# Attention row maxima: four of 32 per unit as a + relu(b - a), single-bank PSUM tiles, and a table of ten phases

## The chip, the core and the metric

The kernel runs on one core of one Trainium2 chip. The metric is the device time of one execution in microseconds (us). Before the change it is 5757.02 us, the median of three runs (5755.38 to 5757.16). The profile is of one further execution, which took 5756.38 us.

## The reference

Four transformer-like layers, A, B, A, B, over a sequence of 2048 rows of 576 values. Each layer adds to x the attention of its normalised input; 32 heads have 18 values each. In layers B all heads share one key and one value head. All is fp32.

```python
def _A_ref(x, wqkv, wo):                    # S = 2048, D = 576, H = 32, Dh = 18
    qkv = (x @ wqkv).reshape(B, S, 3, H, Dh).transpose(2, 0, 3, 1, 4)
    q, k, v = qkv[0], qkv[1], qkv[2]
    scores = jnp.einsum("bhqd,bhkd->bhqk", q, k) * (Dh ** -0.5)
    p = _softmax(scores, axis=-1)
    o = jnp.einsum("bhqk,bhkd->bhqd", p, v)
    return o.transpose(0, 2, 1, 3).reshape(B, S, D) @ wo
x = A_x
x = x + _A_ref(_layernorm(x), A_wqkv, A_wo)
x = x + _B_ref(_layernorm(x), B_wq, B_wk, B_wv, B_wo)   # k, v: one head for all 32
...                                                     # both once more
```

## The kernel before, in words

**Stages of a layer.** Each layer normalises x, projects it to q, k and v on TensorE, runs the attention loop, and projects the result out. Projections split every fp32 operand into a high and a low part and multiply them in TensorE's fp32r format. The attention loop takes most of the time: the 64 **units** of a layer, a unit being one pair of heads `p` (16 pairs) and one block `u` of 512 queries (4 blocks). The instruction order is written out by hand and each engine runs its own queue in that order.

**What a unit does.** The two heads of a pair lie on partitions 0 to 63 (head 0) and 64 to 127 (head 1), so that matmuls of the two heads use different row halves of TensorE's array and run side by side. A unit has

- 32 **m** matmuls (`max_mm`, line 553): 128 queries by 512 keys of one head into PSUM, only to find each query's largest score. VectorE reduces them (line 562). Two m matmuls fill the two banks of one tile `psm` of 1024 columns, and one VectorE instruction takes the maxima of both.
- `max_final` (line 691): the 32 columns of partial maxima (8 query blocks of 4) become 8 negated maxima (VectorE, line 693), split into two parts on GpSimd (`hl`, lines 144 and 697); `max_store` transposes them on VectorE (line 702) and sends them to DRAM, and `max_rows` (line 708) brings them into two spare rows of the query operand in `big`.
- 32 **e** matmuls (`exp_mm`, line 717): 128 keys by 512 queries, with the two spare rows, so that the score minus its maximum comes out. ScalarE takes the exponential (line 721).
- the **PV** matmuls (`pv_block`, line 742): the probabilities times the values, four at a time in four column groups of the array, into one accumulator bank `oacc`. A unit has 4096 columns of them (8 blocks of 512, each for four tiles of probabilities). ScalarE then copies `oacc` out once (line 749), and GpSimd (lines 144, 759, 768, 781) normalises.

**Order.** The maxima of a unit run `LEAD` = 14 steps ahead of its exponentials (a step is an eighth of a unit, 4 m and 4 e). A table `UNIT` gives one period of TensorE's order: each **phase** lists m and e matmuls with their heads, and then a number of PV columns. The table of before has twelve phases. `run_todo` places the small work (DMAs on SyncE's queue, GpSimd steps, loads of the next pair and of later weights) at numbered steps. The first 56 m of a layer are woven into the end of its projections; after its last m, 56 e are left and run without m.

**PSUM.** There are eight banks: two tiles of two banks with tag `m` (`mtile2`), three single banks with tag `e`, and `oacc`. The projections use the same tags; where they want one bank they take the first half of an m tile.

**Staging of weights.** `load_w` brings raw weights into a tile `raw`, and GpSimd splits them one step later (lines 144, 170). In the loop `raw` comes from the two buffers of tag `xh`, in turn.

Of the kernel before, what the change touches and what calls it, by code (L numbers as in the profile page):

```python
# [17 lines left out]
DH = D // H  # L18
# [4 lines left out]
SCALE = DH ** -0.5  # L23

# [38 lines left out]

UNIT = [("m0 m1 e0 e0 e1 m0 m1", 384), ("e0 m1 m0 e1 e0", 352), ("m0 m1 e1 e0 e1 m0 m1", 320), ("m1 e0 e1 m0", 256),
        ("m1 e0 m1 e0 e1", 416), ("e1 m0 m0 e1 m1 e0", 416), ("e1 m0 m1 e0 e1 m0", 384), ("e0 e1 m0 m1 e0", 256),
        ("m1 e0 m0 e1", 128), ("e1 m0 m1 e0", 192), ("e1 m0 m1 e0", 416), ("m0 m1 e1 e0 e1 m1 m0", 576)]
UNIT = [([(o[0], int(o[1])) for o in rows.split()], cols) for rows, cols in UNIT]


@with_exitstack  # L70
def tile_kernel(ctx: ExitStack, tc: tile.TileContext, A_x, A_wqkv, A_wo, B_x, B_wq, B_wk, B_wv, B_wo, out):
# [31 lines left out]
    vbuf = cst.tile([P, NV], F32, name="vbuf")  # L103
    xx = cst.tile([P, 2, 9, 256], F32R, name="xx")
    oacc = psum.tile([P, 512], F32, name="oacc")
    mark = cst.tile([P, 1], F32, name="mark")

# [4 lines left out]
    qk_d = dram.tile([2 * D, 3, S], F32, name="qk_d")  # L112

# [33 lines left out]
    def load_w(c, dsts, srcs, n, hi, lo, spare, raw=None):  # L147


        if raw is None:  # L150
            raw = pool.tile([P, 640], F32, tag="xh", bufs=2, name="raw") if spare else ptile("raw")
# [134 lines left out]
    def out_w(c):  # L286
        ot = ots_[c // 2][:, :, c % 2 * P:(c % 2 + 1) * P]
        ps = mtile2("psn")
        for h in range(2):
            natural(ot, h, ps[:, h])  # L290
        xc = xo[:, c, :].rearrange("p (h n) -> p h n", h=2)
        nc.vector.tensor_tensor(xc, ps[:, :, :288], xc, op=OP.add)
# [85 lines left out]
    for layer in range(4):  # L378
# [11 lines left out]
        def project(T, t, filler=False, half=None, terms=TERMS):  # L390
            t0 = T * 512
            n = 114 if not is_a and t == 4 else P
            if t in half_done:
                ps = half_done.pop(t)
            elif half == 0 and t == 2:
                ps = pair_of[0][:, 1]
            elif half == 0:
                pair_of[t] = mtile2("psq")
                ps = pair_of[t][:, 0]
            else:  # L400
                ps = (etile if filler else mtile)("psq")
# [41 lines left out]
        vts, half_done, pair_of = [], {}, {}  # L443
# [8 lines left out]
        def project_v(c):  # L452
            ps = mtile2("psn")
            for h in range(2):
                natural(xt_of(c), h, ps[:, h])
            return ps[:, :, :288].rearrange("p h (e d) -> p h e d", d=DH)
# [58 lines left out]
        m_open, m_next, m_done, m_count, m_full = [], [0, 0], [0], {}, []  # L515
# [5 lines left out]

        def max_place(a, i):
# [4 lines left out]
            return p, u, i // 2 % 4, i // 8 % 2 * 2 + i % 2  # L527
# [4 lines left out]
        m_banks, n = [], [0, 0]  # L532
        for i in range(0, 4 * ns, 2):
            at_ = []
            for a in m_heads[i:i + 2]:
                p, u, qc, kb = max_place(a, n[a])
                at_.append((p, u, 16 * a + 4 * qc + kb))
                n[a] += 1
            m_banks += [0, 1] if at_[0] < at_[1] else [1, 0]

        def max_mm():

            a, slot = m_heads[m_done[0]], m_banks[m_done[0]]
            p, u, qc, kb = max_place(a, m_next[a])
            q, k = ops(p)
            if (p, u) not in mxs:
                mxs[p, u] = pool.tile([P, 32], F32, name="mx")
            if m_done[0] % 2 == 0:
                m_open.append((mtile2("psm"), []))
            ps, rows = m_open[0]  # L550
            b = 64 * a
            c0 = u * 512 + qc * P
            nc.tensor.matmul(ps[:, slot], q[b:b + KM, c0:c0 + P], k[b:b + KM, kb * 512:(kb + 1) * 512],  # L553
# [344 lines left out]
```

## Time and profile before

| what | value |
|---|---|
| median of three runs | 5757.02 us |
| the profiled execution | 5756.38 us |
| its span (first to last instruction) | 5754.6 us |
| mean granted TensorE clock | 0.998 |
| m matmuls, of 512 columns | 8192 |
| reductions of 1024 columns (line 562) | 4096 |
| exponentials of 512 columns (line 721) | 8192 |

A row of the profile's groups names line, engine, operation, the tiles and shapes, the count, the busy time, the mean duration of one instruction, and the idle time of the engine just before. Instructions of one engine overlap: the busy time counts overlapped time once, so that count times mean can be more than the busy time. TensorE is PE, VectorE DVE, ScalarE ACT, GpSimd POOL, SyncE SP. In a timeline, rows of one group that follow each other are merged: start, length of the merged stretch, and the count behind the x. A PV row of x8 is four fp32 matmuls, each recorded twice.

### The profile page before, as it was taken

The numbers are of one execution on the slowest core, as the hardware profiler recorded it, in microseconds if no ns is written. First come the engines' busy times: TensorE is split into PE (matmuls) and PEld (weight loads), VectorE is DVE, ScalarE is ACT, GpSimd is POOL, SyncE is SP. The second block draws the span as 40 slices with busy tenths as digits, with TensorE's granted clock in tenths as the row PEclk, the third lists the DMA queues.
The fourth block names the chain that finished last, engine by engine and source line by source line (L and its number), as shares of the span: only waits on it lengthen the run. The fifth ranks groups of instructions, "written<-read, shape, count | busy, mean of one in ns | idle before, by whom it ended". The sixth has DMA issues, their size and how long they took to land.

```text
span 5754.6 us, 140964 instructions
## 1 busy us (share of the span) xinstructions
PE 5724.3 (99%) x57758; PEld 2917.8 (51%) x57758; DVE 5121.0 (89%) x5330; ACT 4576.9 (80%) x8864; POOL 1731.4 (30%) x2224
## 2 busy tenths in 40 slices
PE   9999999999999999999999999999999999999999
PEld 8644444444844444444686444444448444444446
DVE  4799999998699999999637999999977999999995
ACT  2588888888378888888625888888882888888885
POOL 3133232323233232323311323232342332323232
PEclk9999999999999999999999999999999999999999
DMA  6311111110420000001243111111114101010002
GB/s 201 106 46 32 35 32 36 32 33 22 127 66 23 23 22 21 20 23 24 59 166 95 40 36 32 36 32 36 29 28 135 52 22 23 22 24 19 23 14 78
DMA packets 250482, 276.93 MB, mean 48 GB/s; under 512 B 131748, under 2 KB 172196, under 8 KB 240116
## 3 DMA queue, kind: packets, MB, share of 16 engines
q1 hardware_dynamic: 249836, 267.92, 16.9%
q8 instruction: 453, 7.42, 0.6%
q14 instruction: 193, 1.58, 0.1%
HBM read 151.24 MB, written 112.56 MB: 46 GB/s over the span
## 4 chain that ended last, share of the span: by engine, by line
PE 97%; POOL 1%; DVE 1%; DMA 1%; ACT 0%; SPq 0%; issue 0%; POOLq 0%; ACTq 0%; DVEq 0%
PE oacc L742 37%; PE pse L717 24%; PE psm L553 23%; PE psn L224 6%; PE psq L405 6%; DVE mx L562 0%; PE ps L216 0%; DMA raw<-in_B_wk_dram 0%; ACT pt L721 0%; POOL big L170 0%; SPq L157 0%; PE oacc L217 0%; POOL os L781 0%; DMA raw<-in_A_wqkv_dram 0%; POOL os L759 0%
## 5 line engine op out<-in xcount | busy, mean ns | idle before, releaser
L562 DVE TENSOR_REDUCE mx<-psm 128x2 f32<-128x1024 f32 x4096 | 4735.7, 1218 | 177.0 <-PE psm L553 161.3
L721 ACT ACTIVATE pt<-pse 128x512 f32<-128x512 f32 x8192 | 4289.5, 606 | 527.1 <-PE pse L717 389.6
L553 PE MATMUL psm<-big 62*128 62x512 f32 x8192 | 2540.9, 452 | 4.2 <-DVE mx L562 3.7
L717 PE MATMUL pse<-big 64*128 64x512 f32 x8192 | 2491.3, 433 | 7.7 <-DMA big<-m_d 5.5
L742 PE MATMUL oacc<-pt,vbuf 128*19 128x64 f32 (+6 forms) x27536 | 1777.8, 361 | 3.5 <-DVE oc L144 3.5
L717 PEld LDWEIGHTS pse<-big 64*128 64x128 f32 x8192 | 1221.7, 184 | 875.9 <-ACT pt L721 700.9
L553 PEld LDWEIGHTS psm<-big 62*128 62x128 f32 x8192 | 1054.0, 184 | 813.4 <-DVE mx L562 640.3
L742 PEld LDWEIGHTS oacc<-pt,vbuf 128*19 128x19 f32 x27536 | 535.4, 97 | 768.5 <-issue 590.9
L144 POOL TENSOR_SCALAR hl<-neg 128x8 fp32r<-128x8 f32 x256 | 50.5, 197 | 2630.8 <-DVE neg L693 2630.8
L768 POOL TENSOR_TENSOR rl<-lt,mone 128x8 f32<-128x8 f32 x256 | 422.1, 1649 | 578.8 <-DMA lt<-os 578.7
L742 PE MATMUL oacc<-pt,vy 128*19 128x128 f32 (+3 forms) x9168 | 594.3, 362 | 0.0
L144 POOL TENSOR_SCALAR os<-oc 32x512 f32<-32x512 f32 x512 | 313.0, 611 | 126.5 <-DVE oc L144 72.5
L781 POOL TENSOR_TENSOR os<-os,rb 96x512 f32<-96x512 f32 x256 | 329.3, 1286 | 21.2 <-DMA rb<-r_d 20.4
L759 POOL TENSOR_TENSOR os<-os,oc 96x512 f32<-96x512 f32 x256 | 328.0, 1281 | 21.3
L742 PEld LDWEIGHTS oacc<-pt,vy 128*19 128x19 f32 x9168 | 195.6, 98 | 271.6 <-issue 212.0
L413 ACT ACTIVATE ev<-psq 128x512 fp32r<-128x512 f32 (+1 forms) x112 | 66.9, 598 | 326.3 <-PE psq L405 236.7
L224 PE MATMUL psn<-wsm,xx 128*128 128x288 f32 x2240 | 307.8, 296 | 0.1
L224 PEld LDWEIGHTS psn<-wsm,xx 128*128 128x128 f32 x2240 | 298.6, 188 | 11.5 <-issue 7.8
L419 DVE TENSOR_TENSOR ev<-psq,ev 128x512 fp32r<-128x512 f32 (+1 forms) x84 | 58.0, 691 | 215.7 <-ACT ev L413 197.4
L405 PE MATMUL psq<-yx,big 128*128 128x512 f32 (+2 forms) x826 | 197.5, 392 | 5.1 <-DVE ev L419 2.5
L405 PE MATMUL psq<-xx,big 128*128 128x512 f32 (+1 forms) x784 | 194.0, 397 | 0.0
L405 PEld LDWEIGHTS psq<-yx,big 128*128 128x128 f32 (+1 forms) x826 | 146.9, 190 | 39.7 <-issue 3.0
(75 smaller groups left out, 1390.5 us busy)
## 6 DMA issues: line engine op xcount, KB each, us to landing
big<-qk_d SPq DMA_DIRECT2D x180, 432.0 KB
qk_d<-ev SPq DMA_DIRECT2D x96, 512.0 KB
qk_d<-ev SPq DMA_DIRECT2D x120, 256.0 KB
rb<-r_d SPq DMA_DIRECT2D x512, 36.0 KB
o_d<-os SPq DMA_DIRECT2D x512, 36.0 KB
m_d<-tr SPq DMA_DIRECT2D x1024, 2.0 KB
o<-o_d SPq DMA_DIRECT2D x64, 256.0 KB
big<-m_d SPq DMA_DIRECT2D x512, 4.0 KB
```

What stands on the lines that cost most here:

```text
L144: eng.tensor_scalar(dst, src, 1.0, 0.0, op0=OP.mult, op1=OP.add)
L224: nc.tensor.matmul(ps, lhs[:, xc, :], wsm[:, wc, h * 288:(h + 1) * 288], start=i == 0, stop=i == len(TERMS) - 1)
L405: nc.tensor.matmul(ps[:n].rearrange("p (u t) -> p u t", u=2)[:, us], w[:, wc, :n], xts[T][:, us, xc, :], start=(xc, wc) == TERMS[0], stop= ...
L413: nc.scalar.activation(ev[0][:n], ps[:n], AF.Copy)
L553: nc.tensor.matmul(ps[:, slot], q[b:b + KM, c0:c0 + P], k[b:b + KM, kb * 512:(kb + 1) * 512], start=True, stop=True)
L562: nc.vector.reduce_max(mxs[p, u][:, r0:r1 + 1:r1 - r0], ps, axis=AX.X)
L717: nc.tensor.matmul(e, k[r:r + KE, kc * P:(kc + 1) * P], q[r:r + KE, u * 512:(u + 1) * 512], start=True, stop=True)
L721: nc.scalar.activation(pt, e, AF.Exp, scale=SCALE)
L742: nc.tensor.matmul(oacc[j:j + DH + 1, cs], v_of(kc)[:, 2 * p + a if is_a else 0, :], pts[p, u, i][:, cs], start=kc < 2 and c0 == 0, stop=k ...
L759: nc.gpsimd.tensor_tensor(t[:96], t[:96], oc[:96], op=OP.add)
L768: nc.gpsimd.tensor_tensor(rl, lts.pop((p, u)), mone, op=OP.pow)
L781: nc.gpsimd.tensor_tensor(t[:96], t[:96], rb[:96], op=OP.mult)
```

## The change

- **Maxima by pairs.** For pairs p > 0, four of the 32 m of a unit (places 9, 16, 24 and 31 of the table's cycle of 32, `UNIT_X`) no longer compute scores of key block 1. They multiply the queries with `kd`, the difference of key block 1 and key block 0, so that PSUM holds b - a. ScalarE writes relu(b - a) into one SBUF tile `relu`. When the scores a of key block 0 of the same queries come, VectorE adds the two and takes the maximum in one call, `tensor_tensor_reduce`, which the built program has as two instructions: one over 512 columns, and one that writes a 128x1 result. It stands for two reductions. The other 24 m of a unit are reduced one by one, 512 columns each. For p = 0 all 32 are. So a unit with p > 0 has 24 reductions of 512, 4 of the new pairs of instructions, and 4 relus.
- **The difference of the keys**, once for each pair in layers A and once in layers B: four DMAs in, five GpSimd instructions on 256 columns, three DMAs out and two back in, at four steps of the loop, into the tile `xx`, which is otherwise unused there.
- **Banks.** Tag `m` becomes three tiles of one bank, tag `e` four, and `oacc` keeps one. Projections use single banks; some VectorE and ScalarE instructions on 576 columns become two on 288.
- **The table** has ten phases. m, e and PV columns of a unit are in sum 32, 32 and 4096, as before.
- **Staging.** The second `xh` buffer is now the one `raw` tile for all weights loaded in the loop, because the first holds `relu`.

```diff
-UNIT = [("m0 m1 e0 e0 e1 m0 m1", 384), ("e0 m1 m0 e1 e0", 352), ("m0 m1 e1 e0 e1 m0 m1", 320), ("m1 e0 e1 m0", 256),
-        ("m1 e0 m1 e0 e1", 416), ("e1 m0 m0 e1 m1 e0", 416), ("e1 m0 m1 e0 e1 m0", 384), ("e0 e1 m0 m1 e0", 256),
-        ("m1 e0 m0 e1", 128), ("e1 m0 m1 e0", 192), ("e1 m0 m1 e0", 416), ("m0 m1 e1 e0 e1 m1 m0", 576)]
+UNIT = [("m1 e0 e1 e0 m1 m0", 512), ("m0 e1 m1 e0 e1 m0", 480), ("e1 m0 m1 e0 e0 m0 e1", 416),
+        ("m1 m0 e1 e0 e1 m0", 224), ("e1 m0 m1 m1 e0", 544), ("m1 m0 e0 e1 e1 m0", 352), ("e0 m1 e1 m0 e0 m1", 416),
+        ("m0 e1 e1 m1 e0 m1 e0", 384), ("m1 m0 e1 e0 m0 e0 e1 m1 m0", 448), ("m0 e1 m1 e0 m1 e0", 320)]
+UNIT_X = (9, 16, 24, 31)
...
-    def mtile2(name):
-        return psum.tile([P, 2, 512], F32, tag="m", bufs=2, name=name)
     def mtile(name):
-        return mtile2(name)[:, 0]
+        return psum.tile([P, 512], F32, tag="m", bufs=3, name=name)
     def etile(name):
-        return psum.tile([P, 512], F32, tag="e", bufs=3, name=name)
+        return psum.tile([P, 512], F32, tag="e", bufs=4, name=name)
...
         def max_mm():
...
+            if p > 0 and (a, qc, kb) in m_diff:
+                nc.tensor.matmul(ps, q[b:b + 3 * DH, c0:c0 + P], kd(p)[b:b + 3 * DH], start=True, stop=True)
+                t = relus[p, u, a, qc] = relu[:, :512]
+                nc.scalar.activation(t, ps, AF.Relu)
+            else:
+                nc.tensor.matmul(ps, q[b:b + KM, c0:c0 + P], k[b:b + KM, kb * 512:(kb + 1) * 512], start=True, stop=True)
+                if kb == 0 and (p, u, a, qc) in relus:
+                    t = relus.pop((p, u, a, qc))
+                    nc.vector.tensor_tensor_reduce(t, ps, t, 1.0, LOWEST, OP.add, OP.max, mx[:, r:r + 1])
+                else:
+                    nc.vector.reduce_max(mx[:, r:r + 1], ps, axis=AX.X)
...
-                nc.vector.reduce_max(mxs[p, u][:, r0:r1 + 1:r1 - r0], ps, axis=AX.X)
...
+        def diff_split(p):
+            n = 4 * DH if is_a else 2 * DH
+            d = dif[:n]
+            hi0, hi1, lo0, lo1 = (xx_flat.bitcast(F32)[:n, 1024 + 256 * i:1280 + 256 * i] for i in range(4))
+            hi, lo = (xx_flat[:n, 2048 + 256 * i:2304 + 256 * i] for i in range(2))
+            nc.gpsimd.tensor_tensor(d, hi1, hi0, op=OP.subtract)
+            nc.gpsimd.tensor_tensor(d, d, lo1, op=OP.add)
+            nc.gpsimd.tensor_tensor(d, d, lo0, op=OP.subtract)
+            copy(nc.gpsimd, hi, d)
+            nc.gpsimd.tensor_tensor(lo, d, hi.bitcast(F32), op=OP.subtract)
...
+        relu, raw = (pool.tile([P, 640], F32, tag="xh", bufs=2, name=n) for n in ("relu", "raw"))
...
+            if p + 1 < NPAIR and (is_a or p == 0):
+                b = max(LEAD, 32 * p - 10)
+                for d, f in ((0, diff_in), (3, diff_split), (5, diff_out), (8, diff_rows)):
+                    at(b + d, f, p + 1)
...
-                at(b - 30, load, c, (2,), nc.gpsimd, nc.gpsimd, True)
-                at(b + 2, load, c, (0,), nc.gpsimd, nc.gpsimd, True)
+                at(b - 30, load, c, (2,), nc.gpsimd, nc.gpsimd, raw)
+                at(b + 2, load, c, (0,), nc.gpsimd, nc.gpsimd, raw)
```

The table with the places of the changed m (X: the difference and its relu; T: the scores to which it is added; in brackets the place in the unit), PV columns at the end of each phase:

```
 1  m1(24) e0 e1 e0 m1(25) m0(26)                    512
 2  m0(27) e1 T1(28) e0 e1 m0(29)                    480
 3  e1 m0(30) m1(31) e0 e0 m0(0) e1                  416
 4  X1(1) m0(2) e1 e0 e1 m0(3)                       224
 5  e1 m0(4) T1(5) m1(6) e0                          544
 6  m1(7) X0(8) e0 e1 e1 m0(9)                       352
 7  e0 m1(10) e1 m0(11) e0 m1(12)                    416
 8  T0(13) e1 e1 m1(14) e0 m1(15) e0                 384
 9  X1(16) m0(17) e1 e0 m0(18) e0 e1 m1(19) m0(20)   448
10  m0(21) e1 T1(22) e0 X1(23) e0                    320
```

More of the change, by code (lines that the diff above doesn't have):

```diff
@@ L394, in project @@
                 ps = half_done.pop(t)
[L395 to L399, printed above, removed]
             else:
@@ L450, in v_trans, with project_v @@
                                   pv.rearrange("p (u e) -> p u e", u=4)[:, :, :DH])
[L452 to L456, printed above, removed]
+        def project_v(c, h):
+            return natural(xt_of(c), h, mtile("psn")).rearrange("p (e d) -> p e d", d=DH)
         def v_dst(c):
@@ L520, in tile_kernel @@
                                    [(1, i, 2) for i in range(4)] + [(1, i, 3) for i in range(4)])
+        m_order, m_diff = [], set()
+        for a in range(2):
+            cycle = [g for rows, _ in UNIT for kind, g in rows if kind == "m"]
+            n = -4 * LEAD % 32
+            own = [(i, i % 32 in UNIT_X) for i in range(n, n + 32) if cycle[i % 32] == a]
+            order = [None] * 16
+            for qc, i in enumerate(i for i, x in enumerate(own) if x[1]):
+                order[i] = qc, 1
+                order[min(j for j, (at_, x) in enumerate(own) if at_ > own[i][0] + 3 and not x and not order[j])] = qc, 0
+                m_diff.add((a, qc, 1))
+            left = [(i // 2 % 4, i // 8 * 2 + i % 2) for i in range(16)]
+            left = [x for x in left if x not in order]
+            m_order.append([x or left.pop(0) for x in order])
         def max_place(a, i):
@@ L546, in max_mm @@
             if (p, u) not in mxs:
[L547 to L551, printed above, removed]
[L552 to L555 removed]
+                mxs[p, u] = pool.tile([P, 32], F32, name="mx") if p == 0 else mx2[u % 2]
```

89 lines of the change are left out of this document (55 added, 34 removed).

## The prediction

> **What bounds the kernel now.** The page's busy shares and its chain of waits come first: which engine is always busy, and which one the end hangs on.
>
> ```profile
> PE 5724.3 (99%) x57758; PEld 2917.8 (51%) x57758; DVE 5121.0 (89%) x5330; ACT 4576.9 (80%) x8864; POOL 1731.4 (30%) x2224
> ...
> PE 97%; POOL 1%; DVE 1%; DMA 1%; ACT 0%; SPq 0%; issue 0%; POOLq 0%; ACTq 0%; DVEq 0%
> PE oacc L742 37%; PE pse L717 24%; PE psm L553 23%; PE psn L224 6%; PE psq L405 6%; DVE mx L562 0%; PE ps L216 0%; DMA raw<-in_B_wk_dram 0%; ACT pt L721 0%; POOL big L170 0%; SPq L157 0%; PE oacc L217 0%; POOL os L781 0%; DMA raw<-in_A_wqkv_dram 0%; POOL os L759 0%
> ```
>
> PE is busy all the time and is 97% of the chain; 84% of the span are the three matmuls of the attention loop. But a busy PE may hide short waits, so I look at a steady stretch of the loop next: busy time by engine, then the `neg` reductions alone, one for each unit.
>
> ```profile
> 420.00:1188.00 768.00, 768.00 (x8331) 347.00 (x8322) 745.13 (x721) 685.71 (x1322) 232.05 (x282) 1.00 0.14 34
> 420.00:1188.00 768.00, 7.00 (x40) 15.94 (x80) 1.00 0.14 34
> ```
>
> The first row gives PE, PEld, DVE, ACT and POOL; the second DVE and POOL for `neg`. 40 units in 768 us are **19.20 us a unit**; in each, DVE is busy 745.13 / 40 = 18.63 us (97%). So two engines are nearly full. Which of the two sets 19.20? I take PE's own cost from its timeline, phase by phase.
>
> ```profile
> 802.57 0.50 PE L717 MATMUL pse<-big 64*128 64x512 f32 x1
> 802.58 0.50 PE L553 MATMUL psm<-big 62*128 62x512 f32 x1
> 802.91 0.39 PE L717 MATMUL pse<-big 64*128 64x512 f32 x1
> 802.92 0.62 PE L553 MATMUL psm<-big 62*128 62x512 f32 x2
> 803.15 0.40 PE L717 MATMUL pse<-big 64*128 64x512 f32 x1
> 803.48 0.90 PE L742 MATMUL oacc<-pt,vbuf 128*19 128x32 f32 x16
> 804.31 0.50 PE L717 MATMUL pse<-big 64*128 64x512 f32 x1
> ...
> 808.18 0.42 PE L742 MATMUL oacc<-pt,vy 128*19 128x128 f32 x8
> 808.53 0.49 PE L717 MATMUL pse<-big 64*128 64x512 f32 x1
> 808.53 0.73 PE L553 MATMUL psm<-big 62*128 62x512 f32 x2
> 808.87 0.40 PE L717 MATMUL pse<-big 64*128 64x512 f32 x1
> 809.19 0.52 PE L742 MATMUL oacc<-pt,vy 128*19 128x192 f32 x8
> ```
>
> Two matmuls, one of each head, start together: a **round**. Six matmuls (three rounds) take 802.57 to 803.48, 0.90 us; four (two rounds) 808.53 to 809.19, 0.66 to 0.67. So a round costs 0.233 us, and m and e of a phase together 0.20 us beside their rounds. The PV of 416 columns (x16: 32, then 384) takes 803.48 to 804.31, 0.83; 128 columns take 808.18 to 808.53, 0.35. That is 1.667 ns a column and 0.137 fixed. A phase therefore has a fixed cost of 0.337 us, whatever is in it.
>
> The old table by this: 12 phases, 35 rounds (7, 5, 7, 4, 5, 6, 6, 5, 4, 4, 4, 7 matmuls; where one head has one more, the round is half empty), 4096 columns: 12 x 0.337 + 35 x 0.233 + 6.83 = **19.03 us**. The measured 19.20 holds only 0.17 us of waits. PE sets the period; DVE follows with 0.57 us idle.
>
> **The change part by part.**
>
> *The table.* Ten phases. Rounds, pairing neighbours of different heads in order: 3, 3, 4, 3, 3, 3, 3, 4, 5, 3 = 34. PE's sum: 10 x 0.337 + 34 x 0.233 + 6.83 = **18.12 us**, 0.91 less than 19.03. Two phases fewer make 0.67 of that, one round fewer 0.23. The difference matmuls have 512 columns as well and change nothing here. The gain comes only if the other engines fit into about 18.1 us.
>
> *VectorE.* Rows for its pitch (start to start without waiting):
>
> ```profile
> 800.56 0.17 DVE L693 TENSOR_REDUCE neg<-mx 128x8 f32<-128x32 f32 x1
> 800.65 2.35 DVE L562 TENSOR_REDUCE mx<-psm 128x2 f32<-128x1024 f32 x2
> 802.91 0.20 DVE L702 STREAM_TRANSPOSE tr<-hl 128x32 f32<-128x32 f32 x1
> 803.35 1.23 DVE L562 TENSOR_REDUCE mx<-psm 128x2 f32<-128x1024 f32 x1 [0.24 <-PE psm L553]
> ...
> 1350.05 14.91 DVE L562 TENSOR_REDUCE mx<-psm 128x2 f32<-128x1024 f32 x13 [0.35 <-PE psm L553]
> ```
>
> Two reductions in 2.35 us, one of them 1.22 long: a pitch of 1.13 for 1024 columns (the run of 13: 1.14). `neg`, with 32 columns, holds the next up for 0.09. A line through the two gives 1.05 ns a column and 0.06 fixed, hence **0.60 us for 512 columns** (0.597). That lies between rows of both sides, so I trust it to 0.03. [...]
>
> `tensor_tensor_reduce` has no row. Its main instruction reads 512 columns from PSUM and 512 from SBUF; below, 0.60 like a reduction of 512; above, 1.13, if it passes its 512 columns at half rate as if they were 1024. Its second, 128x1: below nothing, above 0.44 (transpose to next start). I take 0.60 and 0.09, like the nearest rows, a reduction and `neg`: **0.69**. Sum: 24 x 0.597 + 4 x 0.69 + 0.09 + 0.42 (transpose) = **17.6 us**, a microsecond under before's 18.6. Both ends: 17.2 and 21.1.
>
> *ScalarE* gets four relus.
>
> ```profile
> 801.39 1.58 ACT L721 ACTIVATE pt<-pse 128x512 f32<-128x512 f32 x3
> ...
> 806.59 3.55 ACT L721 ACTIVATE pt<-pse 128x512 f32<-128x512 f32 x7 [0.17 <-PE pse L717]
> ...
> L749 ACT ACTIVATE oc<-oacc 128x512 f32<-128x512 f32 x248 | 153.7, 620 | 0.6 <-PE oacc L742 0.6
> ```
>
> (1.58 - 0.60) / 2 and (3.55 - 0.60) / 6 are both 0.49 us. I take that for a relu too: it reads 512 columns of PSUM and writes 512, like the exponential and the copy (0.61 and 0.62 long), and the built program has one table load, at its head. Sum: 37 x 0.485 = **17.9 us** (before: 33, 16.0). ScalarE had 3 us to spare and now has 0.2.
>
> *Waits that this adds.* Three engines now want 17.6 to 18.1 us of the same period, tied by single banks. I followed the new table through at these prices. Results come 0.50 us after the first start of a phase, 0.40 after later ones. Two places stand out. (1) X at place 23 stands right behind T at 22, and there is one `relu` tile: the relu may not overwrite it until T's add is through. In phase 9 four scores reach DVE from 0.50 on, one 0.60 each, so that place 20 ends at 2.9, 0.65 into phase 10 (phase 9 lasts 2.25); 21 ends at 1.25 and T at 1.94. ACT is done with the exponentials ahead of the relu at about 1.55 and waits 0.4; the exponential behind it waits too. The bank of X is wanted by m at place 26, in the last round of phase 1, 1.57 + 0.57 = 2.14; the relu frees it at about 2.5. PE waits **0.35**. (2) X at 16 and the m at 19 that needs its bank stand in one phase, 1.03 us apart; ACT comes to the relu at about 0.5 and frees the bank at 1.1: **0.1**. Elsewhere banks come back in time: X at 1 and 8 have over 1.4 us, and DVE's backlog stays under its three banks. With that, 18.12 + 0.43 = **18.55 us**. The least would be before's own 0.17, 18.29; the most is a rival below.
>
> *GpSimd, SyncE and the differences.* Nine DMAs and five short POOL instructions in four units; POOL is busy 232 of 768 us, and the issues are steps ahead of their use: nothing. If that cover were gone, `hl` behind `diff_split` would hold DVE's transpose, at most some 2.5 us a pair (five instructions, estimated at 0.5 from 0.61 for 512 columns, the `os` copies).
>
> ```profile
> L144 POOL TENSOR_SCALAR os<-oc 32x512 f32<-32x512 f32 x512 | 313.0, 611 | 126.5 <-DVE oc L144 72.5 <-issue 12.0 <-POOL hl L697 0.4
> ...
> 1331.56 0.41 POOL L144 TENSOR_SCALAR big<-raw 128x256 fp32r<-128x256 f32 x1 [5.58 <-DMA raw<-in_B_wk_dram]
> 1332.05 0.72 POOL L170 TENSOR_TENSOR big<-raw,big 64x256 fp32r<-64x256 f32 x1
> ...
> 1335.30 0.52 SPq L708 DMA_DIRECT2D big<-m_d  x2
> ...
> 1336.74 0.76 PE L717 MATMUL pse<-big 64*128 64x512 f32 x1 [2.50 <-DMA big<-m_d]
> ```
>
> *One raw tile.* Near the end of layers A, POOL waits 5.58 us for weights, more than two steps (2.4 each), the rows of maxima go out late and PE stands 2.50 us. With one tile the next load waits on SP until POOL's split is over, and the maxima's DMAs queue behind it. Nothing below, twice today's stall above (two layers, each a few such waits, some 14 us); I take **+7 us**.
>
> *Pair 0* keeps 32 reductions, each alone: 32 x 0.597 + 0.51 = 19.6 us on DVE, over PE's. 72 of its 128 m stand in the loop, 2.25 units a layer, 9 in all: 0.7 us each, **+6 us**. Projections stay bound by PE; split adds and copies there are hidden behind it: nothing.
>
> *Sum.* 60 units a layer for pairs 1 to 15, 240 in all: 240 x (19.20 - 18.55) = 156 us. From the profiled execution's 5756.4 us (span 5754.6; median of the runs 5757.0): 5756.4 - 156 + 7 + 6 = **5613 us**.
>
> **The rivals.**
>
> *A, the waits dissolve.* A late bank moves the later ones apart, and only before's 0.17 stays: 18.29 us, 240 x 0.91 = 218, **5551 us**. For it: 0.57 us of DVE slack cost PE just 0.17 before. Against it: ACT had 3 us to spare then.
>
> *B, lockstep.* ACT at 17.9 must lose nothing. A relu's wait on DVE, a bank's wait on ACT and DVE's emptiness in the long PV stretches (1.04 us for 544 columns, against 1.8 us of work in three full banks) add up to 0.8: 18.95 us, 60 us won, **5709 us**.
>
> *C, the combined instruction is slow, and the kernel slower.* If it goes at half rate, each pair costs 1.13 + 0.09, and DVE's sum is 14.33 + 4.88 + 0.51 = 19.7; with before's 0.57 of idle 20.3 us, 240 x 1.1 = +262: **6031 us**. It decides from 0.95 us a pair, where the sum is 18.6 as before and PE's gain is cut off. For it: no row shows such an instruction. Against it: a VectorE add of PSUM and SBUF over 512 columns is as long as the line gives for a reduction (0.68):
>
> ```profile
> L419 DVE TENSOR_TENSOR ev<-psq,ev 128x512 fp32r<-128x512 f32 x80 | 55.2, 691 | 204.3 <-ACT ev L413 186.1 <-DMA qk_d<-ev 13.0 <-DMA xo<-in_A_x_dram 2.6
> ```
>
> [...]
>
> *D, the relief is not what counts.* If only the table works, DVE's sum does not matter as long as it is under PE's: that is the forecast itself; the maxima alone, at 19.03 of PE, would give nothing.
>
> **How the numbers follow.** Forecast 0.52 (5570 to 5660), A 0.16, B 0.13, C 0.16; 0.03 for a gain eaten up by more such waits. A measurement can tell some 0.2% (11 us) from no change. Faster: 0.52 + 0.16 + 0.13 = 0.81; same 0.03; slower 0.16. The range goes from A's 5545 to past B, 5740, and leaves C out.
>
> **What would show it.** Right: ten phases with 34 rounds, the same 0.233 and 0.337 in PE's timeline; reductions of 512 at a pitch of 0.60; about 18.5 us between `neg` rows; waits of PE's weight loads on the relu line, mostly in phases 1 and 9. Wrong: the combined pair above 0.95 us; `neg` 19 us apart or more; ACT idle before relus for more than 0.4 us a unit; weight loads in the loop that hold PE for tens of us.

## The result, and the profile after

The changed kernel takes **5910.73 us** (median of four runs, 5908.38 to 5915.58), against 5757.09 for the kernel before on the same chip (5755.38 to 5760.62). The ratio is 1.0267, with a 95% interval of 1.0249 to 1.0285. The forecast was 5613, a gain; it became a loss. The profiled execution spans 5907.6 us, before 5754.6, so 153 us more.

The page's first rows after the change, busy time of the engines and the chain of waits:

```profile
PE 5830.2 (99%) x53790; PEld 2968.2 (50%) x53790; DVE 4938.1 (84%) x9489; ACT 4940.0 (84%) x9840; POOL 1828.0 (31%) x2386
...
PE 96%; DVE 2%; DMA 1%; POOL 1%; issue 0%; ACT 0%; SPq 0%; POOLq 0%; ACTq 0%; DVEq 0%
```

VectorE was relieved as promised: 5121.0 us became 4938.1. But PE, still 99% busy and 96% of the chain, now takes longer for fewer phases. PE counts as busy while a matmul in one half of the array runs and the other half stands still (in phase 1 below, the two m of the last round start at 803.79 and 804.22, not together), so "99%" does not rule out that it waits. The stretch of 30 units in the steady part of the first layer says how much. First the kernel after (busy PE, PEld, DVE, ACT, POOL), then its `neg` rows alone:

```profile
536.40:1121.70 585.30, 584.55 (x5762) 265.27 (x5762) 532.50 (x1021) 558.96 (x1111) 195.37 (x246) 1.00 0.17 42
536.40:1121.70 585.30, 5.27 (x30) 11.96 (x60) 1.00 0.17 42
```

and 30 steady units of the kernel before, `neg` alone:

```profile
512.50:1088.00 575.50, 5.25 (x30) 11.95 (x60) 1.00 0.14 34
```

A unit takes 585.30 / 30 = **19.51 us**, before 19.18; forecast 18.55. In it DVE is busy 532.50 / 30 = 17.75 us (forecast 17.6) and ACT 558.96 / 30 = 18.63 (forecast 17.9, a sum of pitches; the busy time also holds the end of each isolated instruction). The groups show the prices:

```profile
L576 DVE TENSOR_REDUCE mx<-psm 128x1 f32<-128x512 f32 x6272 | 4003.2, 683 | 427.6 <-PE pse L772 202.3
L776 ACT ACTIVATE pt<-pse 128x512 f32<-128x512 f32 x8192 | 4249.2, 634 | 104.8 <-PE pse L772 41.4
...
L569 ACT ACTIVATE relu<-psm 128x512 f32<-128x512 f32 x960 | 594.1, 619 | 161.3 <-PE pse L772 94.3
...
L574 DVE CUSTOM_DVE_ANT_0 relu<-psm,relu 128x512 f32<-128x512 f32 x960 | 654.6, 682 | 2.4 <-PE pse L772 1.2
```

The combined instruction is as long as a reduction of 512 columns (682 and 683 ns), and the next reduction starts 0.60 us after it, beside its second instruction:

```profile
812.34 0.68 DVE L574 CUSTOM_DVE_ANT_0 relu<-psm,relu 128x512 f32<-128x512 f32 x1
812.94 0.08 DVE L574 DVE_READ_ACCUMULATOR2_ANT mx<- 128x1 f32 x1
812.94 1.28 DVE L576 TENSOR_REDUCE mx<-psm 128x1 f32<-128x512 f32 x2
```

So it is not slow. The prices of single instructions are as forecast; what grew are the waits between them. Who waits for whom in those 30 units (total us, times, longest):

```profile
PEld psm L571 <- DVE mx L576: 57.1, 150, 0.7
...
PEld pse L772 <- ACT pt L776: 41.4, 60, 0.8
...
PEld psm L567 <- DVE mx L576: 41.2, 91, 0.7
...
PEld psm L571 <- ACT relu L569: 22.5, 60, 0.5
...
DVE tr L757 <- POOL hl L752: 10.3, 30, 0.4
```

Weight loads run beside matmuls (in these 585.30 us PEld is busy 265.27 and PE 584.55), so only part of each wait moves PE: the four PEld rows are 162.2 us in sum, and PE loses 30 x 1.39 = 41.7 by the next table. Therefore I measured every phase in PE's timeline from its first m or e to the start of its PV, and took medians over 44 units (400 to 1250 us). "Without waits" is (rounds x 0.233) + 0.20, as in the prediction:

| phase | without waits | after | lost |
|---|---|---|---|
| 1 | 0.90 | 1.42 | 0.52 |
| 3 | 1.13 (4 rounds) | 1.13 | 0 |
| 4 | 0.90 | 0.975 | 0.075 |
| 6 | 0.90 | 1.25 | 0.35 |
| 8 | 1.13 (4 rounds) | 1.22 | 0.08 |
| 9 | 1.37 (5 rounds) | 1.74 | 0.37 |
| 2, 5, 7, 10 | 0.90 | 0.89 to 0.91 | 0 |

The sum lost is 0.52 + 0.075 + 0.35 + 0.08 + 0.37 = 1.395 us, and 18.12 + 1.39 = 19.51: the PE sum of the forecast, 18.12, and this one table give the measured period. Three places count.

**Phase 1.** PE, DVE and ACT in the timeline at the end of phase 10 and in phase 1:

```profile
802.22 0.40 PE L567 MATMUL psm<-xx,big 54*128 54x512 f32 x1
...
802.78 0.68 DVE L574 CUSTOM_DVE_ANT_0 relu<-psm,relu 128x512 f32<-128x512 f32 x1
...
803.22 0.50 PE L571 MATMUL psm<-big 62*128 62x512 f32 x1
...
803.57 0.60 ACT L569 ACTIVATE relu<-psm 128x512 f32<-128x512 f32 x1 [0.27 <-DVE mx L574]
...
803.79 0.92 PE L571 MATMUL psm<-big 62*128 62x512 f32 x2
...
804.22 0.18 PEld L571 LDWEIGHTS psm<-big 62*128 62x128 f32 x1 [0.47 <-ACT relu L569]
...
804.65 0.60 PE L797 MATMUL oacc<-pt,vy 128*19 128x480 f32 x4
```

The matmul of X at place 23 starts at 802.22 and is over at 802.62. Its relu starts only at 803.57, when the add of T at place 22 has let go of the one `relu` tile. The bank comes back at 804.22 (the last m's weight load waits 0.47 for it), and the PV starts at 804.65, 1.43 after the phase. This is the wait that the prediction described.

**Phase 6.** DVE and POOL ahead of it:

```profile
808.48 1.30 POOL L157 TENSOR_SCALAR os<-oc 32x512 f32<-32x512 f32 x2 [9.40 <-ACT oc L804]
...
809.84 0.18 DVE L748 TENSOR_REDUCE neg<-mx 128x8 f32<-128x32 f32 x1
809.87 1.28 POOL L814 TENSOR_TENSOR os<-os,oc 96x512 f32<-96x512 f32 x1
...
811.11 0.20 POOL L157 TENSOR_SCALAR hl<-neg 128x8 fp32r<-128x8 f32 x1
...
811.40 0.20 POOL L752 TENSOR_TENSOR hl<-neg,hl 128x8 fp32r<-128x8 f32 x1
...
811.64 0.21 DVE L757 STREAM_TRANSPOSE tr<-hl 128x32 f32<-128x32 f32 x1 [0.35 <-POOL hl L752]
```

`neg` is ready at 810.02, but GpSimd is in the sums of `os` until 811.15; `hl` is through at 811.60, and DVE has stood 0.35 us at the transposition. In the kernel before, `hl` stood ahead of these sums:

```profile
800.82 0.20 POOL L144 TENSOR_SCALAR hl<-neg 128x8 fp32r<-128x8 f32 x1 [10.43 <-DVE neg L693]
801.10 0.20 POOL L697 TENSOR_TENSOR hl<-neg,hl 128x8 fp32r<-128x8 f32 x1
801.39 1.30 POOL L144 TENSOR_SCALAR os<-oc 32x512 f32<-32x512 f32 x2
```

The small work is placed by steps, which the table's e matmuls count out, so another table shifts it on queues that it never mentions. In the runs `old_table` and `banks_alone` below, the changed code with the old table, `hl` again stands ahead of these sums (GpSimd's long wait is `hl` for `neg`, 30 times, up to 12.4 and 12.9 us); in `no_diff`, which keeps the new table, the sums stand ahead of it (the long wait is `os` for `oc`, 30 times, up to 11.1 us).

**Phase 9** has five m and three banks:

```profile
818.54 0.49 PE L567 MATMUL psm<-xx,big 54*128 54x512 f32 x1
818.55 0.50 PE L571 MATMUL psm<-big 62*128 62x512 f32 x1
...
819.07 0.61 ACT L569 ACTIVATE relu<-psm 128x512 f32<-128x512 f32 x1
819.15 0.50 PE L571 MATMUL psm<-big 62*128 62x512 f32 x1
...
819.73 0.30 PEld L571 LDWEIGHTS psm<-big 62*128 62x128 f32 x2 [0.28 <-ACT relu L569]
819.73 0.61 PE L571 MATMUL psm<-big 62*128 62x512 f32 x2
820.27 0.96 PE L797 MATMUL oacc<-pt,vy 128*19 128x224 f32 x16
```

Five rounds should last 5 x 0.233 + 0.20 = 1.37; they take 818.54 to 820.27, 1.73. The fourth m (place 19) wants the bank of X at place 16 back. ScalarE's relu frees it, and the m starts 1.19 after the first instead of 1.03; this is the second wait that the prediction described. The fifth (place 20) starts at 819.85, 1.31 after the first: it wants the bank of place 17 (818.55), which VectorE's reduction frees. In all 31 units between 540 and 1150 us the fourth m is released by the relu and the fifth by VectorE. Of the row for the relu above (22.5 us, 60 times), half of the waits are those of phase 1 (0.47 each) and half these (0.28).

**The bank itself** is seen without other traffic in the first stage, where four m in a row are woven into the projections. After the change, with DVE idle ahead of the first reduction:

```profile
1612.19 0.73 PE L571 MATMUL psm<-big 62*128 62x512 f32 x3
1612.72 2.48 DVE L576 TENSOR_REDUCE mx<-psm 128x1 f32<-128x512 f32 x4 [1.77 <-PE psm L571]
1613.47 0.18 PEld L571 LDWEIGHTS psm<-big 62*128 62x128 f32 x1 [0.99 <-DVE mx L576]
1613.47 0.50 PE L571 MATMUL psm<-big 62*128 62x512 f32 x1 [0.55 <-DVE mx L576]
```

and before, with two tiles of two banks:

```profile
1577.16 0.73 PE L553 MATMUL psm<-big 62*128 62x512 f32 x4
```

Three matmuls find a bank each; the fourth gets the first one's back at 1613.47, **1.28 us** after that was taken: 0.53 until the reduction starts, 0.683 for it, 0.07 to hand over. PE loses 0.55 us, which four banks did not cost.

Where the 153 us lie, by the starts of `neg` (four layers; "first" are the two intervals at the head of each layer's loop, "outside" is all that is not between the first and the last `neg` of a layer):

| | first | rest of the loop | outside |
|---|---|---|---|
| before | 156.1 | 4690.9 | 907.6 |
| after | 195.5 | 4772.5 | 939.6 |

That is 39.4 + 81.6 + 32.0 = 153. The 81.6 is the steady loop; the 32.0 is mostly the waits of the first stage (four layers with 14 groups of four m, 0.55 us each: 31). Of the 39.4, 19.3 us lie in the first interval of each layer (98.6 us in the four layers, before 79.3); `no_diff`, the run below without differences, has 98.7 there, so the differences are not its cause; with a fourth m bank (`m4_e3`) it is 85.2. The other 20.1 us lie in the second interval (96.9, before 76.8), which `no_diff` passes at its steady pace; this is a stall that the new DMAs cause (SyncE's issues, then PE):

```profile
244.30 2.46 SPq L615 DMA_DIRECT2D kd_d<-xx  x3
...
248.65 0.53 SPq L763 DMA_DIRECT2D big<-m_d  x2
...
253.50 1.19 PE L772 MATMUL pse<-big 64*128 64x512 f32 x3 [2.72 <-DMA big<-m_d]
```

At the head of the loop the three DMAs of the first difference stand on SyncE ahead of the rows of maxima, and PE then stands 2.72 us for these rows.

### The profile page after: what moved, and what is told of

Its sections match the earlier page's. It is cut to its first block, busy times and chain, and to the rows that moved or that the text cites. A ratio compares the mean times of both kernels' runs of the same rounds, so it can differ in the third digit from the quotient of the medians.

```text
span 5907.6 us, 140109 instructions
## 1 busy us (share of the span) xinstructions
PE 5830.2 (99%) x53790; PEld 2968.2 (50%) x53790; DVE 4938.1 (84%) x9489; ACT 4940.0 (84%) x9840; POOL 1828.0 (31%) x2386
## 4 chain that ended last, share of the span: by engine, by line
PE 96%; DVE 2%; DMA 1%; POOL 1%; issue 0%; ACT 0%; SPq 0%; POOLq 0%; ACTq 0%; DVEq 0%
PE oacc L797 35%; PE psm L571 23%; PE pse L772 20%; PE psn L240 6%; PE psq L414 6%; PE psm L567 5%; DVE mx L576 1%; PE ps L232 0%; DMA m_d<-tr 0%; DMA big<-m_d 0%; POOL big L186 0%; DMA raw<-in_B_wk_dram 0%; POOL wsm L186 0%; PE oacc L233 0%; SPq L759 0%
## 5 line engine op out<-in xcount | busy, mean ns | idle before, releaser
L576 DVE TENSOR_REDUCE mx<-psm 128x1 f32<-128x512 f32 x6272 | 4003.2, 683 | 427.6 <-PE pse L772 202.3
L776 ACT ACTIVATE pt<-pse 128x512 f32<-128x512 f32 x8192 | 4249.2, 634 | 104.8 <-PE pse L772 41.4
L571 PE MATMUL psm<-big 62*128 62x512 f32 x7232 | 2800.9, 456 | 52.2 <-DVE mx L576 43.1
L772 PE MATMUL pse<-big 64*128 64x512 f32 x8192 | 2353.3, 431 | 9.1 <-DMA big<-m_d 9.1
L797 PE MATMUL oacc<-pt,vbuf 128*19 128x416 f32 (+1 forms) x24560 | 1731.2, 384 | 3.5 <-DVE oc L157 3.5
L571 PEld LDWEIGHTS psm<-big 62*128 62x128 f32 x7232 | 1207.0, 184 | 942.2 <-DVE mx L576 577.5
L569 ACT ACTIVATE relu<-psm 128x512 f32<-128x512 f32 x960 | 594.1, 619 | 161.3 <-PE pse L772 94.3
L574 DVE CUSTOM_DVE_ANT_0 relu<-psm,relu 128x512 f32<-128x512 f32 x960 | 654.6, 682 | 2.4 <-PE pse L772 1.2
L797 PE MATMUL oacc<-pt,vy 128*19 128x288 f32 (+3 forms) x8176 | 567.8, 384 | 0.0
L567 PE MATMUL psm<-xx,big 54*128 54x512 f32 x960 | 455.3, 474 | 0.2
L567 PEld LDWEIGHTS psm<-xx,big 54*128 54x128 f32 x960 | 175.6, 183 | 335.6 <-DVE mx L576 323.3
L836 POOL TENSOR_TENSOR os<-os,rb 96x512 f32<-96x512 f32 x256 | 328.3, 1282 | 23.6 <-DMA rb<-r_d 22.5
```

The source lines that it names most:

```text
L567: nc.tensor.matmul(ps, q[b:b + 3 * DH, c0:c0 + P], kd(p)[b:b + 3 * DH], start=True, stop=True)
L569: nc.scalar.activation(t, ps, AF.Relu)
L571: nc.tensor.matmul(ps, q[b:b + KM, c0:c0 + P], k[b:b + KM, kb * 512:(kb + 1) * 512], start=True, stop=True)
L574: nc.vector.tensor_tensor_reduce(t, ps, t, 1.0, LOWEST, OP.add, OP.max, mx[:, r:r + 1])
L576: nc.vector.reduce_max(mx[:, r:r + 1], ps, axis=AX.X)
L772: nc.tensor.matmul(e, k[r:r + KE, kc * P:(kc + 1) * P], q[r:r + KE, u * 512:(u + 1) * 512], start=True, stop=True)
```

## The experiments

**Theory.** The prices are right. The loss lies in tiles that return too late, above all the three single m banks: a bank is away for 1.25 us (matmul 0.5, reduction 0.68, handing over 0.07), not for the 0.60 of DVE's pitch. **Rivals**: the relief of DVE is the culprit (the relus crowd ScalarE, the differences crowd GpSimd and SyncE), or the table alone is, or the splitting of the bank pairs alone.

Times are medians; each ratio is to the kernel before, timed with it on the same chip (medians of 5755.8 to 5757.1 us), with its 95% interval. "A unit" is the mean of 30 steady units, as above. Kernels that were timed once have no interval.

### Parts of the change by themselves

**no_diff**: all else of the change, but all 32 maxima of a unit from reductions of 512.

```diff
-UNIT_X = (9, 16, 24, 31)
+UNIT_X = ()
...
-            if p + 1 < NPAIR and (is_a or p == 0):
+            if UNIT_X and p + 1 < NPAIR and (is_a or p == 0):
```

> The changed kernel without differences: no relus, no key differences and their DMAs, all 32 maxima of every unit reduced alone from single banks, ten-phase table. VectorE's sum is 32 x 0.60 + 0.5 = 19.6 us a unit. Late banks: 19.6 plus 0.5 to 0.9 of idle, 20.1 to 20.5 us, 6050 to 6150 us, so that the relus are a gain of 140 to 240 us on top of a loss by single banks. Rival (ScalarE, filled by the relus, is what holds the changed kernel at 19.5): relieved of them the unit stays at 19.6 to 19.7, 5900 to 5960 us.

6134.21 us, 1.0658 (1.0642 to 1.0674); a unit 20.54. So the four maxima by relu *win* 1.03 us a unit in this frame, and the ScalarE, GpSimd and SyncE work that comes with them costs less than that. DVE is busy 598.29 / 30 = 19.94 us of each unit (the prices give 32 x 0.597 + 0.51 = 19.6), which alone is over the 19.18 of before: in single banks a reduction of 512 columns cost it 0.60 here, in pairs of banks one of 1024 cost 1.13 before.

**old_table**: the changed kernel with the old table of twelve phases, differences kept. Timed once.

```diff
-UNIT = [("m1 e0 e1 e0 m1 m0", 512), ("m0 e1 m1 e0 e1 m0", 480), ("e1 m0 m1 e0 e0 m0 e1", 416),
...
+UNIT = [("m0 m1 e0 e0 e1 m0 m1", 384), ("e0 m1 m0 e1 e0", 352), ("m0 m1 e1 e0 e1 m0 m1", 320), ("m1 e0 e1 m0", 256),
...
```

> The changed kernel with differences, relus and single banks, but the old table of twelve phases (TensorE's own sum 19.03 us a unit; the places of the differences fall elsewhere). Late banks: phases of four m in a row lose 0.3 to 0.5 us each, and there are four of them in the old table: 20.0 to 20.6 us a unit, 6030 to 6170 us. Rival (VectorE's relief by the relus is what counts, any table does): about 19.5 us, 5911 us.

6298.90 us (before 5755.77); a unit 21.16, more than both sides had expected (6170 us and 20.6 at most).

**banks_alone**: both edits, so that of the change only the banks are left, with what goes with them (reductions of 512 one by one, split copies, one raw tile). Timed once.

```diff
-UNIT_X = (9, 16, 24, 31)
+UNIT_X = ()
...
-UNIT = [("m1 e0 e1 e0 m1 m0", 512), ("m0 e1 m1 e0 e1 m0", 480), ("e1 m0 m1 e0 e0 m0 e1", 416),
...
+UNIT = [("m0 m1 e0 e0 e1 m0 m1", 384), ("e0 m1 m0 e1 e0", 352), ("m0 m1 e1 e0 e1 m0 m1", 320), ("m1 e0 e1 m0", 256),
...
```

> The changed kernel without differences and with the old table of twelve phases: only the banks differ from the kernel before (three single m banks, four e banks, 8192 reductions of 512 columns). VectorE's sum is 19.6 us a unit and TensorE's 19.03. Late banks: 20.0 to 20.6 us a unit, 6000 to 6160 us, a loss by itself. Rival (single banks give PE finer release and cost nothing beyond VectorE's sum): 19.6 to 19.8 us, 5870 to 5930 us.

6289.03 us (before 5756.72); a unit 21.12, 1.94 over the kernel before: this is the largest price of the change, and also above what was expected (6160 us and 20.6 at most). With the old table the relus bring nothing (21.16 against 21.12), since DVE's sum is not the limit there (busy 17.96 us a unit with them, 19.92 without): the three phases with four m last 1.71 to 1.82 us (medians of both runs) instead of 1.13. The expectations had put 0.3 to 0.5 us on each such phase and had counted four of them; 0.57 to 0.69 came. The new table alone wins 0.58 (21.12 to 20.54), and the relus on top of it 1.03.

**table_alone**: the kernel before with the new table only (two tiles of two m banks, three e banks, pairs reduced together).

```diff
-UNIT = [("m0 m1 e0 e0 e1 m0 m1", 384), ("e0 m1 m0 e1 e0", 352), ("m0 m1 e1 e0 e1 m0 m1", 320), ("m1 e0 e1 m0", 256),
...
+UNIT = [("m1 e0 e1 e0 m1 m0", 512), ("m0 e1 m1 e0 e1 m0", 480), ("e1 m0 m1 e0 e0 m0 e1", 416),
...
```

> The kernel before with the ten-phase table and nothing else: two-bank m tiles, 4096 reductions of 1024 columns, no relus. TensorE's own sum falls from 19.03 to 18.12 us a unit, VectorE keeps 18.63. Late banks (the theory: the period is set by when single banks come back, not by an engine's sum): VectorE at 18.6 plus some idle bounds it, 18.8 to 19.2 us a unit, 5660 to 5757 us. Rival (the table itself is bad, whatever the banks): 19.5 us a unit as in the changed kernel, 5830 us or more.

6707.36 us, 1.1653 (1.1635 to 1.167); a unit 23.05. My expectation (5660 to 5757) missed by far. The page's chain of this run and, for comparison, that of m4_e3 below:

```profile
PE 66%; DVE 28%; ACT 3%; issue 3%; DVEq 0%; POOL 0%; DMA 0%; SPq 0%; ACTq 0%; POOLq 0%
```

```profile
PE 69%; ACT 22%; DVE 4%; issue 3%; DMA 1%; POOL 0%; SPq 0%; ACTq 0%; POOLq 0%
```

Here the chain runs through VectorE: 27 of its 28% are the reductions of 1024 columns (line 562). A tile of two banks comes back only after both of its m and a reduction of 1024 columns (1.22 us in the profile before), and the new table has phases with three and five m. The exponentials, for which the three e banks wait, are at most ScalarE's 3%; in m4_e3 ScalarE has 22%. So by this chain it is the pair tiles that I had not counted, more than the e banks; no run separates the two.

**m4_e3**: the changed kernel with four single m banks and three e banks.

```diff
-        return psum.tile([P, 512], F32, tag="m", bufs=3, name=name)
+        return psum.tile([P, 512], F32, tag="m", bufs=4, name=name)
...
-        return psum.tile([P, 512], F32, tag="e", bufs=4, name=name)
+        return psum.tile([P, 512], F32, tag="e", bufs=3, name=name)
```

> The changed kernel with four m banks and three e banks for three and four; nothing else. A bank is taken for about 1.25 us from the start of its matmul (0.50, a reduction of 0.69, a semaphore). Late banks: with a fourth m bank the five m of phase 9 and the four in a row of the first stage no longer wait, phases 1, 6 and 9 lose less: 19.5 goes to 18.7 to 19.0 us a unit, 5911 to 5740 to 5800 us. Rival (ScalarE is full and needs its four banks): waits of the e matmuls take their place, 5900 us or more.

6531.53 us, 1.1346 (1.1329 to 1.1363). This, too, I had expected to help (5740 to 5800). Its steady units, and what waited in them:

```profile
563.20:1234.00 670.80, 5.26 (x30) 12.09 (x60) 1.00 0.15 37
```

```profile
PEld pse L772 <- ACT pt L776: 169.5, 270, 1.2
...
DVE mx L576 <- PE psm L571: 101.5, 203, 0.8
```

A unit takes 670.80 / 30 = 22.36 us. The waits of e matmuls for the exponential are four times those of the changed kernel (169.5 against 41.4): with ten phases, up to four e in one, and three e banks, PE waits for ScalarE (22% of the chain above), and VectorE then for PE. So, as far as these runs show, the table needs the fourth e bank, that leaves three m banks of the eight that every kernel here uses, single ones make all maxima too dear for VectorE (19.94 us a unit in `no_diff`), and only then do the relus pay. The three parts of the change hang together, and the theory "more m banks would mend it" falls.

### Waits taken away one by one

**two_relus**: relus alternate between `relu` and the idle `raw` tile in pairs 3 to 13.

```diff
-                t = relus[p, u, a, qc] = relu[:, :512]
+                t = relus[p, u, a, qc] = (relu, raw)[r_next[0] % 2 if 3 <= p < 14 else 0][:, :512]
+                r_next[0] += 1
```

> The changed kernel with two relu tiles in turn for pairs 3 to 13 (the second is the raw tile, unused then), 176 of 240 units; nothing else changed. Late banks: the relu at place 23 no longer waits for the add at 22, the 0.52 us that TensorE loses in phase 1 goes in those units: 176 x 0.5 = 88 us, 5820 us. Rival (ScalarE is full): the wait turns up elsewhere, 5890 to 5911 us.

5844.94 us, 1.0153 (1.0136 to 1.017): 66 us under the changed kernel (88 expected). Phase 1 falls from 1.42 to 1.04 and a unit to 19.14. Among its waits the row of weight loads for the relu falls from 22.5 us (60 times) to 8.5 (30 times): phase 1's are gone, phase 9's have stayed, and so has that of DVE for `hl`, at 10.3.

**nm3**: the transposition and its DMAs one step later.

```diff
-NM_AT = 2
+NM_AT = 3
```

> The changed kernel with the transposition of the maxima one step (about 2.4 us) later in the order (NM_AT 3 for 2); nothing else. Late banks: VectorE no longer stands before the transposition until GpSimd, busy with the os sums, has made hl; the 0.35 us that TensorE loses in phase 6 goes, 240 x 0.35 = 84 us, 5825 us. Rival (ScalarE is full): 5890 to 5911 us.

5849.15 us, 1.0163 (1.0148 to 1.0178): 62 us under the changed kernel (84 expected). Phase 6 falls from 1.25 to 1.01 and a unit to 19.28. DVE's wait for `hl` is gone, that for the relu has stayed (21.6 us). Together, the two runs show two separate causes.

**four**: both, and the fourth m of each group in the first stage in an e bank, and the last two steps of the first difference in a layer two and three steps later.

```diff
-            mx, ps = mxs[p, u], mtile("psm")
+            mx, ps = mxs[p, u], (etile if i < 4 * LEAD and i % 4 == 3 else mtile)("psm")
...
-                for d, f in ((0, diff_in), (3, diff_split), (5, diff_out), (8, diff_rows)):
+                for d, f in ((0, diff_in), (3, diff_split), (5 if p else 7, diff_out), (8 if p else 11, diff_rows)):
```

> The changed kernel with four repairs: two relu tiles in turn (pairs 3 to 13), the transposition one step later, the fourth m of each four in a row in the first stage into an e bank, and the first pair's differences out two and back three steps later. Late banks: the first two give 66 and 62 us alone, and add up because they sit in different phases; the third gives some 0.55 us for each of 14 groups a layer, 25 to 30 us; the fourth up to 20 us: 5911 - 66 - 62 - 27 - 15 = 5741 us (5720 to 5770), near the kernel before. Rival (ScalarE is full at 18.6 busy of 19.1): no more than the better of the two, 5800 to 5845 us.

5713.45 us, 0.9925 (0.991 to 0.9939): the gains add up (0.37 and 0.23 us a unit alone, 0.60 together), the kernel is faster than before, and by more than expected (5720 at best). A unit takes 18.91; phases 1 and 6 last 1.04 and 1.01. By the split of the table above it has 162.5, 4651.6 and 897.6 us: the first stage is mended, and with it the first interval (78.2 us in the four layers). The stall of the first difference is not gone, though: the second and third intervals of the four layers take 84.3 and 86.3 us, after the change 96.9 and 79.2. In the first layer it has only moved one unit on: the third interval is 25.9 us, and PE stands 3.33 us at 260.32 for the rows of maxima (`big<-m_d`).

**three_m4**: as `four`, but without the e bank in the first stage and with four m and three e banks.

```diff
-        return psum.tile([P, 512], F32, tag="m", bufs=3, name=name)
+        return psum.tile([P, 512], F32, tag="m", bufs=4, name=name)
...
-        return psum.tile([P, 512], F32, tag="e", bufs=4, name=name)
+        return psum.tile([P, 512], F32, tag="e", bufs=3, name=name)
```

> The changed kernel with two relu tiles in turn (pairs 3 to 13), the transposition one step later, the first pair's differences later, and four m banks with three e banks. Late banks: phases 1, 6 and 9 at TensorE's own cost or near it, 18.4 to 18.7 us a unit: 5630 to 5700 us, faster than the kernel before. Rival (ScalarE is full): not under 18.9 us a unit, 5745 us or more.

6458.06 us, 1.1221 (1.1203 to 1.124). It rests on the same wrong theory as m4_e3, and misses (5630 to 5700) for the same reason.

**four_x2**: as `four`, but the second relu tile is a free part of `xx` (for all pairs p > 0) instead of `raw`.

```diff
-                t = relus[p, u, a, qc] = relu[:, :512]
+                t = relus[p, u, a, qc] = (relu[:, :512], xx_flat[:, 2560:3072])[r_next[0] % 2]
+                r_next[0] += 1
...
-                    nc.vector.tensor_tensor_reduce(t, ps, t, 1.0, LOWEST, OP.add, OP.max, mx[:, r:r + 1])
+                    nc.vector.tensor_tensor_reduce(t, ps, t.bitcast(F32), 1.0, LOWEST, OP.add, OP.max, mx[:, r:r + 1])
```

> The four repairs, but with the second relu tile in free columns of xx and used by every pair after the first (240 units instead of 176); relu and sum are rounded to fp32r there, which only moves the shift that the softmax cancels. Late banks: the 64 units that still stood at 19.27 come to 18.90, 64 x 0.37 = 24 us: 5713 to 5690 us. Rival (the second tile brings new waits of its own, between xx's uses): 5713 us or more.

**5689.78 us**, 0.9882 (0.9865 to 0.9898), the best of all kernels here. Its steady units, and phases 6 and 1 in the timeline (PE and its weight loads):

```profile
515.00:1082.40 567.40, 567.29 (x5762) 267.87 (x5762) 533.81 (x1021) 554.41 (x1111) 195.69 (x246) 1.00 0.17 44
```

```profile
707.31 0.50 PE L572 MATMUL psm<-big 62*128 62x512 f32 x1
...
707.89 0.18 PEld L572 LDWEIGHTS psm<-big 62*128 62x128 f32 x1
707.90 0.49 PE L572 MATMUL psm<-big 62*128 62x512 f32 x1
...
708.32 0.49 PE L798 MATMUL oacc<-pt,vbuf 128*19 128x352 f32 x4
...
716.96 0.49 PE L572 MATMUL psm<-big 62*128 62x512 f32 x1
...
718.00 0.60 PE L798 MATMUL oacc<-pt,vy 128*19 128x480 f32 x4
```

Phase 6 lasts 707.31 to 708.32, 1.01 us, and phase 1 716.96 to 718.00, 1.04, a little over 0.90. In phase 6, 0.09 of that lies at the end: the weights of the last m come only at 707.89, with the matmul itself, which is then 0.49 long instead of 0.40, and the PV starts 0.42 after it instead of 0.33. ScalarE is busy 554.41 / 30 = 18.48 us of 18.91: beside PE it is now the fullest engine, with VectorE behind it (17.79). That it would be the next bound is not tested.

**four_x2_ph9**: as `four_x2`, with the fifth m of phase 9 moved into phase 10.

```diff
-        ("m0 e1 e1 m1 e0 m1 e0", 384), ("m1 m0 e1 e0 m0 e0 e1 m1 m0", 448), ("m0 e1 m1 e0 m1 e0", 320)]
+        ("m0 e1 e1 m1 e0 m1 e0", 384), ("m1 m0 e1 e0 m0 e0 e1 m1", 448), ("m0 e1 m0 m1 e0 m1 e0", 320)]
```

> As four_x2, with the fifth m of phase 9 moved to the head of phase 10 (four m in each; 34 rounds as before). A bank is gone for 1.25 us from the start of its matmul, and a phase of four rounds starts its last at 0.80: each phase with four m waits some 0.35 to 0.45 for its fourth, 0.75 in the two where phase 9 alone lost 0.37. Late banks: 0.4 us a unit worse, 240 x 0.4 = 96 us, about 5785 us. Rival (five m in one phase are what hurts, spreading them helps): 5690 - 240 x 0.3 = 5620 us.

5837.76 us, 1.0142 (1.0121 to 1.0162); a unit 19.54. Slower was expected, but by 95 us (5785), not by 148. Phase 9 became 1.62 and phase 10, now with four m, 1.71 us instead of 0.90. With three m banks, the phases with four m lasted 1.62 to 1.82 us in all three runs that have them (this one, `old_table`, `banks_alone`); moving the fifth m only added a second such place. The expectation also miscounted: by the prediction's own way of pairing, phase 9 keeps five rounds and phase 10 now has four, 35 in all and not 34. At 0.233 us a round that is some 56 us over 240 units, about the 53 us by which it missed. The longer phases agree with the round trip of a bank (1.28 us in the first stage) as the cause.

## Why the prediction was wrong

**The failed step is "Waits that this adds"**: 0.43 us a unit was forecast, 1.39 came (19.51 - 18.12). The forecast had two waits, 0.35 and 0.1 (0.45 in sum, of which it used 0.43). Phase 1 came 0.17 dearer and phase 9 0.27; phase 6 (0.35) and phases 4 and 8 (0.155) were put at nothing. Over the rest of the loop that is the measured +81.6 instead of the forecast -156: 238 of the 296 us by which the span missed. Point by point:

- *The table.* Right. PE's prices (0.233 a round, 0.337 a phase) hold, and phases 2, 3, 5, 7 and 10 run at them. 18.12 us plus the measured waits is the period.
- *VectorE, ScalarE.* Right in the prices. Reductions and combined instructions follow each other at 0.60 us; the second instruction (0.08 long) lies beside the next, so a pair costs 0.60 and not 0.69. DVE's 17.75 us are close to the forecast 17.6. ScalarE's pitches hold as well (medians from start to start: 0.48 us for an exponential, 0.49 for a relu); that it is busy 0.7 us more than forecast I put down to instructions that stand alone, which are 0.6 long.
- *Rival C* is refuted by that price: with one source in PSUM and one in SBUF, the combined instruction takes 0.60 us from start to start for 512 columns, as a reduction does, and not the 1.13 that C had put.
- *Waits that this adds, (1).* The mechanism was right, as two_relus shows, its price short: 0.52 instead of 0.35, of which a second tile takes away 0.38. 0.09 of the rest is a late weight load, behind which the PV starts 0.43 after the matmul (804.22 to 804.65) and not 0.33.
- *(2).* Right, and near in price: the m at place 19 comes 0.16 late (1.19 instead of 1.03), forecast 0.1.
- *"Elsewhere banks come back in time… DVE's backlog stays under its three banks".* Wrong. I treated a bank as free at VectorE's pitch. It is gone for matmul, the reduction's whole length and the handing over, some 1.25 us (1.28 in the first stage). In phase 9 the fifth m (place 20) waits for that, 0.28 late, and with the late weight load at the end the phase loses 0.37 instead of 0.1.
- *GpSimd, SyncE and the differences: "nothing".* Wrong, in two ways. I feared for `hl` behind `diff_split`, and it was the sums of `os` that moved ahead of it, in every unit: 0.35 us in phase 6, of which nm3 takes away 0.24. And the DMAs of the first difference delay the rows of maxima at the head of the layers, 20.1 us in the four.
- *"Projections stay bound by PE: nothing".* Wrong for the first 56 m of a layer, 14 groups of four in three banks at 0.55 us or more each. This and the point before are the other 58 us of the miss (39.4 + 32.0 against the 13 that pair 0 and the raw tile were given). Of these 13, the 7 for the one raw tile do not show: the longest unit near the end of the layers A takes 26.0 and 24.6 us before, 25.1 and 23.5 after. The 6 for pair 0 are not separated by any run here.
- *Rival B, lockstep,* had the right kind of loss and 18.95 us a unit, which would still have been faster. The walk that gave it was too kind to the banks. Its other leg, ScalarE that must lose nothing, is not tested; once the two waits are mended ScalarE is busy 18.48 of 18.91.
- *Rival D.* The relus count: without them a unit is 20.54 instead of 19.51. VectorE's sum is one thing in pairs of banks (18.6 us) and another in single banks (19.6 by the prices, 19.94 busy in `no_diff`); I set their relief against the former.

Left open: why three e banks cost as much as they do with this table (22.36 against 19.51 us), since that was read from the waits and the chain only and not tried with another order of e; the share of the pair tiles and of the e banks in table_alone; the 0.37 of phase 9, which the last run moved but did not mend, and the 0.08 each of phases 4 and 8, which were not looked into.

## What to carry to other kernels

A PSUM bank was away here for the whole way round (matmul, the full length of the instruction that empties it, handing over: 1.28 us), not for the consumer's pitch (0.60): count how many matmuls of a phase start within that time, and compare with the banks. When a table that paces everything is changed, list the order of the small work on every queue before and after; what moved ahead of what cost here nearly as much as the tile that I had looked at (62 and 66 us). A change that loses can hold a gain: a relu tile and PSUM banks that came back late, and small work in the wrong place, hid 1.2% against the kernel before.

## What the runs showed of the hardware

- `tensor_tensor_reduce` with one operand in PSUM and one in SBUF, both fp32, 512 columns: 0.682 us long, 0.60 from start to start, like a plain reduction; the read of its accumulator (0.08 us) starts with the next reduction (both at 812.94) and does not hold it up.
- A relu of 512 PSUM columns takes ScalarE 0.62 us, like an exponential (0.63).
- A busy PE hides waits: 99% before, 99% after, with 1.39 us of waits in each 19.51.
